# The second layer's early choice in two column groups, ScalarE alone for three accumulator copies, and other widths for two hot experts

## The chip, the cores and the metric

The kernel runs on one core of a Trainium2 chip. A time is the device time of one launch in microseconds (us). The engines of the core work in parallel, each through its own instructions in a fixed order: TensorE (PE; its weight loads are PEld), VectorE (DVE), ScalarE (ACT), GpSimd (POOL) and SyncE (SP, which only issues DMAs here). TensorE accumulates into PSUM; ScalarE and VectorE bring the results into SBUF.

## The reference

Linear attention over 4 x 8 heads of 576 tokens with a head size of 64, then two mixture-of-experts (MoE) layers on the 2304 tokens of 512 values. Each MoE layer chooses one of 8 experts per token, the second with a capacity of 576 tokens per expert:

```python
def _moe_ref(x, w_gate, w1, w2):
    logits = x @ w_gate
    expert_idx = np.argmax(logits, axis=1)
    ...
        xe = x[mask]
        h = np.maximum(xe @ w1[e], 0.0)          # 512 -> 1024
        ye = h @ w2[e]                           # 1024 -> 512
        out[mask] = gate_w[mask, None] * ye

# second layer, the same with
    cap = N // E * 2                             # 576
    for i in range(N):
        e = expert_idx[i]
        if counts[e] < capacity: ...             # later tokens of a full expert give zeros
```

For the inputs that are timed, the first layer's experts have 275, 263, 320, 346, 271, 298, 310 and 221 tokens, the second layer's 477, 159, 320, 248, 144, 524, 259 and 173 (worked out with the reference on its own inputs).

## The kernel before

**Blocks.** All matrix work of a layer is cut into blocks of tokens of one expert, run one after the other by `moe` (L1421). A block of width w has a phase 1 (hidden values, `phase1_prods` L1222, tile `hps`: 8 groups of 12 matmuls, each group called fc 0 to 7) and a phase 2 (`phase2` L1247, accumulators `acc`: again 8 groups of 12). Values are split in a high and a low part and three products are added (`prods`, L1205, lines L1211 to L1213), so 192 matmuls of w columns make a block. In layer one the blocks are 128 (inside the attention stage), 224, 320, 312, 300, 276, 272, 264 and 224 wide, counted 0 to 8. The first layer's rows lie in 23 columns of up to 128 rows: column 0 is block 0, block 5 (276 wide) starts at column 12, block 7 (264) at 18. `LAYOUT2` gives the widths of the second layer in the order of the experts' token counts that are left after an early block of 256 tokens of the "hot" expert, the one with most tokens in the columns that the early choice sees.

**Block forms in layer two.** A block whose width is a multiple of 128 is computed by rows: phase 2 takes the hidden values as the stationary operand and 512 columns of w2 as the moving one (48 matmuls for a width of 256), and its output is scaled by ScalarE and scattered by one DMA per 128 tokens (`still_tile`, L1278). Any other width is "turned": 96 matmuls of w columns, VectorE transposes of the four accumulators, VectorE products with the gate and one scatter on POOL per 32 tokens (`turn_out`, L1374).

**Order of the work around the matmuls.** After each group fc the function `slot` (L1451) issues, in this order: the outputs of the block before (`outs`), a split of one weight tile for what comes next (`feed.pump`: ScalarE makes the high part, L1105, VectorE the low part, L1108), steps of a routing generator, and in phase 2 one step of the next block's input (`xs`). For the last five blocks of layer one a tile of that input is a VectorE transpose (`xw`, L1162), then ScalarE's high part (`xh`, L1195), then VectorE's low part (`xl`, L1199). A generator is run by credit: `run(us)` adds us and steps until the credit is used up; a bare `yield` costs 0.27, `yield PE_WAIT` 1.54.

**The early choice of layer two** (`early(1)`, L861) works on the first 18 columns of the first layer's output in a single group: maximum and one-hot (`chosen`), counts by two matmuls (`prefix`, L615/L616), the hot expert, ranks, one-hot tables (`lo` L929, `high_hot`), a matmul gather of indices (`index`, L666) and the indirect DMAs that fetch the first 256 tokens (L1137). It is stepped in phase 2 of block 7 (0.4 of credit a slot, `THEN0`) and in block 8 (0.7 a slot in phase 1, `THEN1`). The code already has a branch for a second group of columns, which takes the hot expert from the first group and adds ranks by two small matmuls.

**Accumulator copies.** When a block of layer one ends, `evac` (L1314) copies its four accumulators to `yt`: numbers 0 and 2 on ScalarE (L1321), 1 and 3 on VectorE (L1319). Matmuls with an identity and the gate's weights (`yps`, L1341) turn `yt` into rows in the next block's phase 1; ScalarE (`y`, L1345) and VectorE (`l`, L1346) read them, and two PSUM tiles take turns.

Of the kernel before, what the change touches and what calls it, by code (L numbers as in the profile page):

```python
# [27 lines left out]
GROUPS = ((0, 4), (4, 9), (9, 13), (13, 18))  # L28
# [22 lines left out]
TA = 1, WA // 128  # L51


LAYOUT1 = [[224], [320], [312], [300], [276], [272], [264], [224]]
LAYOUT2 = [[256], [256, 268], [320], [260], [176], [160], [144], [256]]
RANKS1 = [0, 1, 2, 3, 4, 5, 6, 7]
RANKS2 = [0, 1, 2, 3, 5, 6, 7, 4]

# [47 lines left out]
def tiles_of(w):  # L106
    return (w + 127) // 128
# [18 lines left out]

L1, L2 = Layout(LAYOUT1, TA[0]), Layout(LAYOUT2, TA[1])
NT = max(L1.nt, L2.nt)
XWMAX = max(w for ws in LAYOUT1 + LAYOUT2 for w in ws)
NCMAX = max(NCOL, L1.cols)  # L130


EARLY = ((GROUPS[1][1],), (TA[0] + L1.base[-2],))
NEARLY = [g[-1] for g in EARLY]


def constants():
# [18 lines left out]
    put("rev", 7 - e)  # L156
    for n in sorted({NCOL, L1.cols, N // 128, *sum(EARLY, ())}):
        put(f"carry{n}", np.tile(np.arange(n) > 0, E))
# [17 lines left out]
class Kernel:  # L176
# [411 lines left out]
    def chosen(self, m, c0, c1, d, oh):  # L588
# [4 lines left out]
        first = self.firsts[m][:, c0:c1]  # L593
        A3 = [128, n, E]
        mx = self.t([128, n], F32, "mx")
        V.tensor_reduce(out=mx, in_=lg, axis=AX.X, op=ALU.max)
        V.tensor_tensor(out=d, in0=lg, in1=bc(mx, 2, A3), op=ALU.subtract)
        yield
        w = self.t(A3, F32, "w")
        V.scalar_tensor_tensor(out=w, in0=d, scalar=0.0, in1=first, op0=ALU.is_equal, op1=ALU.mult)  # L600
        V.tensor_reduce(out=mx, in_=w, axis=AX.X, op=ALU.max)
        yield
        V.tensor_scalar(out=mx, in0=mx, scalar1=0.5, scalar2=None, op0=ALU.max)
        V.tensor_tensor(out=oh, in0=w, in1=bc(mx, 2, A3), op=ALU.is_equal)
        yield PE_WAIT
# [166 lines left out]
    def lead(self):  # L772
# [4 lines left out]
        er = self.er[0] = {}  # L777
        A3, AE = [128, n, E], [128, E, n]
        eq = t(A3, F16, "ohe")
        d = t(A3, F32, "da")  # L780
# [80 lines left out]
    def early(self, m):  # L861


        nc, V, t = self.nc, self.nc.vector, self.t
        groups = EARLY[m]
        ncol = groups[-1]
        er = self.er[m] = {}
        val = (self.tok1, self.slot2)[m][:, 0:ncol]
        oh = t([128, ncol, E], F16, "ohe")
        d = t([128, ncol, E], F32, "da")  # L870
        own = t([128, ncol], F16, "owna")
        sel = t([128, ncol], F32, "sel")
        tl = t([128, ncol], F16, "tla")
        lo = self.xp.tile([128, 128, ncol], F16, tag="lo", name="loa")
        hv = self.rp.tile([128, 2, TA[1], ncol], F16, tag="hva", name="hva")
        hot = t([128, E], F32, "hot0")
        er["sel"], er["d"], er["hot"], er["hot_low"], er["hot_high"] = sel, d, hot, lo, hv
        for c0, c1 in zip((0,) + groups, groups):
            n = c1 - c0
            s = slice(c0, c1)  # L880
            A3 = [128, n, E]
            yield from self.chosen(m, c0, c1, d[:, s], oh[:, s])
            if c0 == 0:
                run, pf = yield from self.prefix(oh[:, s], n)
                key = t([128, E], F32, "key")
                V.scalar_tensor_tensor(
                    out=key, in0=run[:, :, n - 1], scalar=8.0, in1=self.c("rev"), op0=ALU.mult, op1=ALU.add
                )
                top = t([128, 1], F32, "top")
                V.tensor_reduce(out=top, in_=key, axis=AX.X, op=ALU.max)  # L890
                yield
                V.tensor_scalar(out=hot, in0=key, scalar1=top, scalar2=None, op0=ALU.is_equal)
                he = t([128, E], F32, "he")
                V.tensor_tensor(out=he, in0=hot, in1=self.c("e"), op=ALU.mult)
                ordf = t([128, 1], F32, "orda")
                V.tensor_reduce(out=ordf, in_=he, axis=AX.X, op=ALU.add)
                er["ordi"] = t([128, 1], I32, "ordia")
                V.tensor_copy(out=er["ordi"], in_=ordf)
                yield
            w = t(A3, F32, "w")  # L900
            V.tensor_tensor(out=w, in0=oh[:, s], in1=bc(hot, 1, A3), op=ALU.mult)
            with nc.allow_low_precision("zeros and ones"):
                V.tensor_reduce(out=own[:, s], in_=w, axis=AX.X, op=ALU.add)
            yield
            rank = t([128, n], F32, "rank")
            if c0 == 0:
                V.tensor_tensor(out=w, in0=w, in1=pf.rearrange("p e c -> p c e"), op=ALU.mult)
                V.tensor_reduce(out=rank, in_=w, axis=AX.X, op=ALU.add)
            else:
                before = self.psum()[:, 0:c1 + n]  # L910
                nc.tensor.matmul(out=before[:, c1:], lhsT=self.triw, rhs=own[:, s], start=True, stop=True)
                nc.tensor.matmul(out=before[:, 0:c1], lhsT=self.onew, rhs=own[:, 0:c1], start=True, stop=True)
                self.hold = True
                yield
                run = t([128, c1], F32, "runa")
                V.tensor_tensor_scan(
                    out=run, data0=self.c(f"carry{c1}")[:, 0:c1], data1=before[:, 0:c1], initial=0.0,
                    op0=ALU.mult, op1=ALU.add,
                )
                V.tensor_tensor(out=rank, in0=before[:, c1:], in1=run[:, s], op=ALU.add)  # L920
                self.hold = False
            yield
            V.scalar_tensor_tensor(
                out=sel[:, s], in0=rank, scalar=float(WA), in1=own[:, s], op0=ALU.is_lt, op1=ALU.mult
            )
            low, tla = yield from self.low_high(rank, n, "")
            V.tensor_tensor(out=tl[:, s], in0=tla, in1=sel[:, s], op=ALU.mult)
            yield
            V.tensor_tensor(  # L929
                out=lo[:, :, s], in0=self.iotaw[:, :, s], in1=bc(low, 1, [128, 128, n]), op=ALU.is_equal  # L930
            )
            yield 0.1 * n
            self.high_hot(tl[:, s], val[:, s], n, TA[1], hv[:, :, :, s])
            yield PE_WAIT
        yield from self.index(m, er, lo, hv, ncol, TA[1], "a", self.blocks[m][0].gather)
# [375 lines left out]

        return [turn, logits]

    def evac(self, acc, w):  # L1314
        nc = self.nc
        yt = self.yt_tile(w)
        for dc in range(DC):
            if dc % 2:
                nc.vector.tensor_copy(out=yt[:, dc, 0:w], in_=acc[dc][:, 0:w])  # L1319
            else:  # L1320
                nc.scalar.activation(out=yt[:, dc, 0:w], in_=acc[dc][:, 0:w], func=ACTF.Copy)  # L1321
        return yt
# [98 lines left out]
    def moe(self, m, then=None, follow=None, fin=None):  # L1421

        blocks, feed = self.blocks[m], self.feed[m]
# [4 lines left out]
        def run(l, n=99):  # L1428
            for _ in range(n):
                if l:  # L1430
                    l.pop(0)()

        def settle(*gens):
            for g in gens:
                while self.hold:
                    g.step()

        for k, b in enumerate(blocks):
            if m == 0 and k < 1:
                continue  # L1440
            j, w = b.j, b.w
            nb = blocks[k + 1] if k + 1 < len(blocks) else None
            nx = nb or follow
            gen = fin if nb else (then or Steps(iter(())))
            also = then if then and k == len(blocks) - 2 else None
            own, ahead = 8 * j + 8, 8 * j + (12 if nb and nb.j != j else 8)
            if k and nb:
                nb.gather()
# [28 lines left out]
            else:  # L1477
                for fc in range(FC):
# [4 lines left out]
                    elif fc:  # L1483
                        slot(fc % 2 or j == 0 or not nb, own, RATES[m][0] if nb else THEN1)
            run(outs)
            feed.pump(4, own)
            settle(gen)
            self.psum, self.spare = lambda: self.ph.tile([128, 512], F32, tag="h", name="sp"), "h"
# [2 lines left out]
            if rows and not nb and w > 128:  # L1491
                self.nc.gpsimd.drain()
                for t in range(w // 128):
                    acc = self.pa.tile([128, 512], F32, tag="a", name="acc")
# [8 lines left out]
            acc = [self.pa.tile([128, 512], F32, tag="a", name="acc") for _ in range(w // 128 if rows else DC)]  # L1503
# [19 lines left out]
                    xs.extend(nb.x_steps())  # L1523
            if k == 1:
                fin.run()
            settle(gen)
            if also:
                settle(also)
            if rows and m:
                for t in range(w // 128):  # L1530
                    self.still_tile(acc[t], b.rt, b.t0 + t)
            elif rows:
                outs.extend(self.still_rows(acc[0], b.rt, b.t0, b.col))
            elif b.turned:
                outs.extend(self.turn_out(acc, w, b.rt, b.t0))
            else:
                yt = self.evac(acc, w)
                for t in range(tiles_of(w)):
                    outs.extend(self.out_tile(m, yt, w, b.rt, b.t0, t, b.col))
            run(xs)  # L1540
# [167 lines left out]
    def run(self):  # L1708
        nc, tc, ctx = self.nc, self.tc, self.ctx
        self.pools()  # L1710
        self.hold = False
        self.tags, self.lp = {"hv", "pv"}, None
        self.view, self.turning = 0, 1
        self.er, self.rt = [{}, {}], [{}, {}]
# [222 lines left out]
```

## Time and profile before

| what | value |
|---|---|
| median of 3 runs | 582.75 us (581.17 to 585.8) |
| profiled execution, its own time | 584.3 us |
| its span, first to last instruction | 582.5 us |
| TensorE busy | 552.8 us, 95% of the span |
| VectorE / ScalarE / GpSimd busy | 57% / 42% / 31% |
| mean granted TensorE clock | 0.986 of full |

The busy time of TensorE counts pipelined matmuls as one stretch, so short waits between two matmuls hide in it. In the timeline a number in brackets with an arrow is the idle time of the engine before the instruction, and what ended it. In the table of stretches (block 5's phase 2 is 233.8 to 245.8, block 8's two phases 300.5 to 319.3 and 319.3 to 336.5) PEclk is the granted clock of TensorE, as a share of full.

### The profile page before, as it was taken

To read this page: it belongs to the slowest core of one execution; us is meant where nothing else is said; L and a number is where in the kernel's file an instruction comes from. 1 tells how busy PE (TensorE), PEld (TensorE's weight loads), DVE (VectorE), ACT (ScalarE), POOL (GpSimd) and SP (SyncE) were. 2 spreads that over 40 slices of the span, in tenths; PEclk is the share of its full clock that TensorE was granted. 3 is DMA by queue.
4 is the path that set the end of the run, shared out by engine and by line. 5 is a ranking of instruction groups with operands and counts; after the bars stand their busy time and mean duration, and the time that the engine had idled before them with its cause. 6 is when DMAs were issued, how large, how long until landed. Compare 5 with 4: busy or idle time off the path is not lost.

```text
span 582.5 us, 10758 instructions
## 1 busy us (share of the span) xinstructions
PE 552.8 (95%) x4130; PEld 525.1 (90%) x4130; DVE 330.2 (57%) x741; ACT 243.8 (42%) x421; POOL 182.4 (31%) x187
## 2 busy tenths in 40 slices
PE   8898898999999999999998999999999999999995
PEld 6887776998999999999987998989899999989994
DVE  0466983467867576767688586275147662211370
ACT  0456622436455555564645342244243532111440
POOL 1032225066625243433000101203322726543341
PEclk8999899999999999999999898999999999999998
DMA  9996746055556465656555434236234655768631
GB/s 305 399 381 217 264 144 193 3 178 168 179 172 205 157 203 172 213 176 200 175 181 166 134 111 167 72 93 234 88 101 153 202 188 177 257 238 265 242 127 39
DMA packets 34231, 106.89 MB, mean 184 GB/s; under 512 B 6665, under 2 KB 6795, under 8 KB 34172
## 3 DMA queue, kind: packets, MB, share of 16 engines
q1 hardware_dynamic: 24432, 81.90, 41.8%
q0 software_dynamic: 7072, 19.48, 10.7%
q10 hardware_dynamic: 2667, 4.75, 2.4%
q8 instruction: 34, 0.56, 0.4%
q14 instruction: 26, 0.20, 0.1%
HBM read 91.77 MB, written 14.60 MB: 183 GB/s over the span
## 4 chain that ended last, share of the span: by engine, by line
PE 69%; DVE 15%; issue 6%; ACT 5%; DMA 2%; POOL 1%; POOLq 0%; SPq 0%; ACTq 0%; DVEq 0%; another core or an unknown queue 0%
PE hps L1211 8%; PE hps L1212 8%; PE hps L1213 8%; PE acc L1211 7%; PE acc L1212 7%; PE acc L1213 7%; PE acc L1209 5%; PE hps L1209 4%; PE yps L1341 3%; DVE w1l L1108 3%; DVE w2l L1108 2%; PE xps L1187 2%; PE kv L368 2%; PE o L400 2%; PE sp L666 1%
## 5 line engine op out<-in xcount | busy, mean ns | idle before, releaser
L1211 PE MATMUL hps<-xh,w1h 128*128 128x256 f32 (+9 forms) x480 | 141.5, 295 | 1.0 <-ACT xh L1195 0.6
L1212 PE MATMUL hps<-xl,w1h 128*128 128x256 f32 (+9 forms) x480 | 139.0, 290 | 0.6 <-DVE xl L1199 0.5
L1213 PE MATMUL hps<-xh,w1l 128*128 128x256 f32 (+9 forms) x480 | 138.6, 289 | 0.0
L1232 ACT ACTIVATE hh<-hps 128x256 fp32r<-128x256 f32 (+12 forms) x144 | 54.4, 380 | 150.1 <-PE hps L1213 97.6
L1211 PE MATMUL acc<-hh,w2h 128*128 128x224 f32 (+8 forms) x352 | 104.6, 297 | 0.1
L1212 PE MATMUL acc<-hl,w2h 128*128 128x224 f32 (+8 forms) x352 | 103.0, 293 | 0.8 <-issue 0.8
L1213 PE MATMUL acc<-hh,w2l 128*128 128x224 f32 (+8 forms) x352 | 103.1, 293 | 0.0
L1211 PEld LDWEIGHTS hps<-xh,w1h 128*128 128x128 f32 x480 | 91.0, 190 | 3.0 <-issue 1.5
L1212 PEld LDWEIGHTS hps<-xl,w1h 128*128 128x128 f32 x480 | 91.1, 190 | 1.7 <-DVE xl L1199 1.3
L1213 PEld LDWEIGHTS hps<-xh,w1l 128*128 128x128 f32 x480 | 91.1, 190 | 0.0
L1234 DVE SCALAR_TENSOR_TENSOR hl<-hps,hh 128x256 fp32r<-128x256 f32 (+9 forms) x120 | 51.7, 436 | 63.7 <-ACT hh L1232 54.7
L1148 POOL DMA_INDIRECT xg<-x1d,gi x54 | 54.9, 1016 | 77.5 <-DVE xw L1162 63.5
L1108 DVE TENSOR_TENSOR w2l<-raw,w2h 128x1024 fp32r<-128x1024 f32 x52 | 66.2, 1276 | 19.2 <-ACT w2h L1105 18.1
L1396 POOL DMA_INDIRECT out_dram<-y,gi x44 | 50.5, 1149 | 70.9 <-DVE y L1392 56.8
L1108 DVE TENSOR_TENSOR w1l<-raw,w1h 128x1024 fp32r<-128x1024 f32 x52 | 64.0, 1248 | 13.6 <-ACT hh L1232 7.8
L1213 PEld LDWEIGHTS acc<-hh,w2l 128*128 128x128 f32 x352 | 67.2, 191 | 0.9 <-issue 0.9
L1211 PEld LDWEIGHTS acc<-hh,w2h 128*128 128x128 f32 x352 | 67.3, 191 | 0.3
L1212 PEld LDWEIGHTS acc<-hl,w2h 128*128 128x128 f32 x352 | 67.3, 191 | 0.2 <-issue 0.2
L1105 ACT ACTIVATE w2h<-raw 128x1024 fp32r<-128x1024 f32 x52 | 54.6, 1053 | 5.6 <-ACT y L1345 4.8
L1105 ACT ACTIVATE w1h<-raw 128x1024 fp32r<-128x1024 f32 x52 | 53.4, 1049 | 0.6 <-DMA raw<-in_moe_w_dram 0.5
L1137 POOL DMA_INDIRECT xg<-x2d,gi x21 | 20.0, 952 | 48.3 <-DVE gi L677 33.9
L1195 ACT ACTIVATE xh<-xps 128x512 fp32r<-128x512 f32 (+7 forms) x23 | 11.7, 512 | 45.3 <-PE xps L1187 31.2
(315 smaller groups left out, 818.9 us busy)
## 6 DMA issues: line engine op xcount, KB each, us to landing
raw<-in_moe_w_dram SPq DMA_DIRECT2D x104, 512.0 KB
w<-in_moe_w_dram SPq DMA_DIRECT2D x24, 512.0 KB
x1d<-xs POOLq DMA_DIRECT2D x4, 1056.0 KB
qkv<-in_k_dram SPq DMA_DIRECT2D x8, 512.0 KB
qkv<-in_v_dram SPq DMA_DIRECT2D x8, 512.0 KB
qkv<-in_q_dram SPq DMA_DIRECT2D x8, 512.0 KB
x2d<-y ACTq DMA_DIRECT2D x15, 256.0 KB
xg<-x1d,gi POOLq DMA_INDIRECT x59
```

What stands on the lines that cost most here:

```text
L1105: self.nc.scalar.activation(out=h, in_=t, func=ACTF.Copy)
L1108: self.nc.vector.tensor_tensor(out=l, in0=t, in1=h, op=ALU.subtract)
L1137: self.nc.gpsimd.indirect_dma_start(out=xg[:n], out_offset=None, in_=(self.X1, self.X2)[m][0:rows], in_offset=bass.IndirectOffsetOnAxis(ap ...
L1148: self.nc.gpsimd.indirect_dma_start(out=xg[:, g], out_offset=None, in_=(self.X1, self.X2)[m].rearrange("n (q x) -> (n q) x", q=4), in_offs ...
L1209: nc.tensor.matmul(out=out, lhsT=a[0], rhs=b[0], start=start, stop=stop)
L1211: nc.tensor.matmul(out=out, lhsT=a[0], rhs=b[0], start=start, stop=False)
L1212: nc.tensor.matmul(out=out, lhsT=a[0], rhs=b[1], start=False, stop=False)
L1213: nc.tensor.matmul(out=out, lhsT=a[1], rhs=b[0], start=False, stop=stop)
L1232: nc.scalar.activation(out=hh[:, fc, :], in_=ps, func=ACTF.Relu)
L1234: nc.vector.scalar_tensor_tensor(out=hl[:, fc, :], in0=ps, scalar=0.0, in1=hh[:, fc, :], op0=ALU.max, op1=ALU.subtract)
L1341: nc.tensor.matmul(out=ps[:n, j, :], lhsT=yt[:, dc, 128 * t:128 * t + n], rhs=self.iwg[:, dc, :], start=True, stop=True)
L1396: self.nc.gpsimd.indirect_dma_start(out=out, out_offset=bass.IndirectOffsetOnAxis(ap=rt["si4"][:, g - g0, t0 + t:t0 + t + 1].bitcast(U32), ...
```

## The change

The early choice of layer two takes its 18 columns in two groups, 12 and then 6. It is stepped in phase 2 of blocks 5, 6 and 7 instead of 7 alone, and a group begins only when the outputs of its columns have been issued (`self.done`). The hot expert is now the one that leads in the first 12 columns. `settle` steps the generators in turn until none holds a matmul result. ScalarE alone copies the accumulators of blocks 6, 7 and 8. Layer two's hot expert gets a rest of 268 (was 256) and the next expert 256 and 224 (was 256 and 268). The constant table gains the row of 96 values that a scan over 12 columns needs.

```diff
-LAYOUT2 = [[256], [256, 268], [320], [260], [176], [160], [144], [256]]
+LAYOUT2 = [[268], [256, 224], [320], [260], [176], [160], [144], [256]]
...
-EARLY = ((GROUPS[1][1],), (TA[0] + L1.base[-2],))
+EARLY = ((GROUPS[1][1],), (TA[0] + L1.base[-4], TA[0] + L1.base[-2]))
...
@@ early
             A3 = [128, n, E]
+            while self.done < c1:
+                yield
             yield from self.chosen(m, c0, c1, d[:, s], oh[:, s])
...
-    def evac(self, acc, w):
+    def evac(self, acc, w, alone=False):
...
-            if dc % 2:
+            if dc % 2 and not alone:
                 nc.vector.tensor_copy(out=yt[:, dc, 0:w], in_=acc[dc][:, 0:w])
...
@@ moe
         def settle(*gens):
-            for g in gens:
-                while self.hold:
-                    g.step()
+            while self.hold:
+                for g in gens:
+                    if g and self.hold:
+                        g.step()
...
-            also = then if then and k == len(blocks) - 2 else None
+            also = then if then and len(blocks) - 5 < k < len(blocks) - 1 else None
...
             run(outs)
+            if m == 0:
+                self.done = b.col
             feed.pump(4, own)
...
-            settle(gen)
-            if also:
-                settle(also)
+            settle(gen, also)
...
-                yt = self.evac(acc, w)
+                yt = self.evac(acc, w, k > len(blocks) - 4)
...
-        self.hold = False
+        self.hold, self.done = False, 0
```

## Rows read from the trace of the kernel before

**Rows 1.** The page, busy time of each engine, share of the span and instructions.
```profile
PE 552.8 (95%) x4130; PEld 525.1 (90%) x4130; DVE 330.2 (57%) x741; ACT 243.8 (42%) x421; POOL 182.4 (31%) x187
```

**Rows 2.** Stretches: us, busy us (instructions) of PE, PEld, DVE, ACT, POOL; PEclk, DMA, GB/s.
```profile
233.80:245.80 12.00, 12.00 (x98) 12.00 (x97) 8.59 (x12) 6.26 (x9) 5.97 (x6) 1.00 0.65 204
...
300.50:319.30 18.80, 15.31 (x140) 14.49 (x139) 16.38 (x50) 9.78 (x21) 0.00 (x0) 1.00 0.53 173
319.30:336.50 17.20, 16.81 (x142) 16.38 (x141) 9.67 (x27) 7.08 (x13) 1.93 (x2) 0.90 0.49 157
```

**Rows 3.** Timeline of DVE in block 5's phase 2: start, us, instruction, [idle before].
```profile
236.49 1.22 DVE L1108 TENSOR_TENSOR w1l<-raw,w1h 128x1024 fp32r<-128x1024 f32 x1
237.63 0.70 DVE L1162 STREAM_TRANSPOSE xw<-xg 128x512 f32<-128x512 f32 x1
239.13 0.75 DVE L1199 SCALAR_TENSOR_TENSOR xl<-xw,g,xh 128x512 fp32r<-128x512 f32 x1 [0.79 <-ACT xh L1195]
240.08 1.23 DVE L1108 TENSOR_TENSOR w1l<-raw,w1h 128x1024 fp32r<-128x1024 f32 x1 [0.20 <-ACT w1h L1105]
...
245.57 0.36 DVE L1199 SCALAR_TENSOR_TENSOR xl<-xw,g,xh 128x64 fp32r<-128x64 f32 x1 [0.42 <-issue]
...
247.66 0.79 DVE L1319 COPY yt<-acc 128x276 f32<-128x276 f32 x2
```

**Rows 4.** Timeline of PE: the second matmul of blocks 6 and 7.
```profile
245.98 0.39 PE L1212 MATMUL hps<-xl,w1h 128*128 128x272 f32 x1
...
273.73 0.39 PE L1212 MATMUL hps<-xl,w1h 128*128 128x264 f32 x1 [0.35 <-DVE xl L1199]
```

**Rows 5.** Groups of DVE instructions, 291 to 320 us: busy us, mean ns.
```profile
L929 DVE TENSOR_TENSOR loa<-iotaw,low 128x2304 f16<-128x2304 f16 x1 | 1.4, 1420 | 0.0
...
L597 DVE TENSOR_TENSOR da<-aux,mx 128x144 f32<-128x144 f32 x1 | 0.3, 308 | 0.0
...
L886 DVE SCALAR_TENSOR_TENSOR key<-run,ct 128x8 f32<-128x8 f32 x1 | 0.2, 157 | 0.0
```

**Rows 6.** Waits of PE, 240 to 336.5 us: us in total, times, longest.
```profile
PE yps L1341 <- DVE l L1346: 1.8, 2, 1.4
PE yps L1341 <- DVE yt L1319: 1.1, 1, 1.1
PE sp L666 <- DVE hva L659: 0.9, 1, 0.9
```

**Rows 7.** Timelines of ACT and DVE: accumulator copies of block 7.
```profile
300.49 0.65 ACT L1321 ACTIVATE yt<-acc 128x264 f32<-128x264 f32 x2
...
304.21 0.76 DVE L1319 COPY yt<-acc 128x264 f32<-128x264 f32 x2
```

**Rows 8.** Busy time by stretch: 3.3 us early in block 8's phase 2.
```profile
320.10:323.40 3.30, 3.30 (x18) 3.30 (x17) 1.81 (x9) 0.01 (x1) 1.93 (x2) 0.50 0.57 186
```

**Rows 9.** Timelines of POOL and PE: gathers, and what reads them.
```profile
98.15 0.95 POOL L1137 DMA_INDIRECT xg<-x1d,gi  x1 [0.30 <-issue]
...
101.92 1.05 POOL L1179 TENSOR_TENSOR xr<-xg 128x512 f32<-128x512 f32 x1 [0.42 <-DMA xg<-x1d,gi]
...
320.44 0.98 POOL L1137 DMA_INDIRECT xg<-x2d,gia  x1 [46.80 <-DMA raw<-in_moe_w_dram]
...
326.23 0.63 PE L1187 MATMUL xps<-ct,xg 128*128 128x128 f32 x4
```

**Rows 10.** Busy time by stretch: 224 columns; layer two's 256, 256, 268 (two phases).
```profile
329.80:333.80 4.00, 4.00 (x38) 4.00 (x37) 4.00 (x5) 2.44 (x5) 0.00 (x0) 1.00 0.64 207
368.90:392.20 23.30, 23.30 (x153) 21.30 (x152) 13.46 (x39) 9.40 (x17) 3.99 (x4) 1.00 0.30 95
392.20:416.20 24.00, 24.00 (x158) 21.55 (x157) 9.36 (x15) 9.37 (x18) 4.89 (x5) 1.00 0.50 170
416.20:428.10 11.90, 11.90 (x97) 11.90 (x96) 2.97 (x7) 3.54 (x9) 5.90 (x6) 1.00 0.40 123
428.10:441.50 13.40, 13.40 (x110) 13.19 (x109) 7.73 (x12) 5.77 (x8) 1.84 (x2) 1.00 0.45 138
```

## Prediction

> **What bounds the kernel now.** First the busy table: TensorE is busy 95% of the span, VectorE 57% [rows 1]. So only two kinds of edit can pay: less matmul work, or an end to stretches in which TensorE waits. The table of stretches shows where these are. Phase 2 of block 5 is full: 12.00 of 12.00 us [rows 2]. In phase 1 of block 8 TensorE is busy 15.31 of 18.80 us and VectorE 16.38: there VectorE is the bound [rows 2]. The list of waits puts names to it: 1.1 us until VectorE copies an accumulator, 1.4 us (and twice a little) until VectorE's gate sums free a PSUM tile, 0.9 us until the one-hot table of the early choice is there [rows 6]. And behind that last wait 3.3 us of phase 2 ran at a granted clock of 0.50, that is at 1.2 GHz of 2.4 [rows 8].
>
> The second thing to see is how close VectorE is to being the bound in the earlier blocks, though it is busy only 8.59 of 12.00 us there [rows 2]. The timeline of block 5's phase 2 shows a chain: weight split 236.49, transpose 237.63, then VectorE stands 0.79 us until ScalarE has made the high part, low part 239.13, next weight split 240.08 [rows 3]. One input tile takes 3.6 us (240.08 - 236.49), three tiles and their weights nearly the whole phase. The last low part begins at 245.57 and takes 0.36, so it ends at 245.93; the matmul that reads it starts at 245.98 [rows 3, 4]. One block later that matmul already waits, 0.35 us [rows 4]. So what is put into VectorE's queue in phase 2 of blocks 5 and 6 ahead of these parts comes out as a wait of TensorE, except what fits into the 0.8 us holes.
>
> **The change part by part.** I add up differences against the profiled execution (584.3 us, span 582.5; 1.55 above the median of 582.75) and apply them to the median.
>
> *Early choice, first group.* Credit of 0.4 a slot fixes what is issued where. In block 5: fc 0 two steps (four operations on 12 x 8 = 96 values), fc 1 one step, fc 5 the two matmuls, the scan and an add, fc 6 two tiny ones, fc 7 six. Durations: 144 values take 0.308 us, 8 values 0.157 [rows 5], so 96 values about 0.26 (estimate, on that line). Ahead of the last low part and not in a hole: 4 x 0.26 + (0.16 + 0.26) + 0.6 (scan and add) = 2.1 us. The matmul had no slack, so block 6 starts its second matmul 2.1 us late. Behind it, fc 7's operations (1.2 us) and the weight split precede block 5's accumulator copies on VectorE, which are still shared there: 247.66 [rows 3] becomes some 251.2, the first copy is done at 251.6, and `yps` wants it after two groups of 1.5 us behind 248.0, at 251.1: 0.45 us more. In block 6: fc 0 two operations (0.55), fc 1 seven small ones (7 x 0.16 = 1.1), fc 2 the one-hot table, 1.42 x 12/18 = 0.95 us [rows 5], of which 0.8 fits the hole, fc 5 two (0.3): 0.55 + 1.1 + 0.15 + 0.3 = 2.1 us, all of it on top of the 0.35. Sum for the first group: **+4.65 us**. Bounds: 0, if the chain has slack that I don't see, and 6.
>
> *Second group.* Six columns, in block 7's phase 2, whose next block has two input tiles and no wait at its start: nothing. What is left of it (ranks, tables, 1.75 us of VectorE with a table of 0.5) runs in block 8's fc 1 and fc 2. Two more pairs of small matmuls and one pair fewer: **+0.3 us** of TensorE (the pair of before and one `x18` gather stay).
>
> *Copies by ScalarE alone.* Two copies take 0.65 us on ScalarE, 0.76 on VectorE [rows 7]; VectorE began its own only at 304.21, 3.7 us after ScalarE's 300.49 [rows 7], because early steps stood before them. Four in a row on ScalarE end some 1.3 us after the block's end, and `yps` comes after two groups of 1.3 us: the wait of 1.1 us goes, **-1.1**. ScalarE has nothing else due until the first `hh`. At block 8's own end the same takes some **-0.4** of the small waits.
>
> *Block 8's other waits.* The gate sums of the second output tile stand in VectorE's queue behind the first w2 split and the steps of fc 1. These steps are 1.75 us now against 1.4 before, while TensorE comes 1.1 us earlier: by my walk through the two queues the sums are done at about 309.9 and TensorE wants the tile at 307.95, a wait of 2.0 in place of 1.4: **+0.6**. The index matmuls move from fc 7 to fc 4 and find their table: **-0.9**. With no wait in front of phase 2 the clock should stay: 3.3 us at half rate lose half, **-1.6**.
>
> *What is late next.* The input steps of layer two follow four slots after the gather is issued. The gather moves forward, but its index is read on VectorE behind the queue, at about 316.4; POOL takes it at some 317.2 (0.8 allowed). How long it takes to land is not shown directly: a product that waited for a gather issued at 98.15 began at 101.92, 3.8 us [rows 9], and the one issued at 320.44 was read at 326.23 without a wait, so at most 5.8 [rows 9]. TensorE comes to these transposes at about 320.3, the rows at 321.0 to 323.0: a wait of 0.7 to 2.7, I take **+1.5**, nearer to the gather that is seen waited for.
>
> *Widths.* The hot expert of the first 12 columns is the one with 524 tokens (299 there against 260 of the one with 477; over 18 columns it was 436 against 446), so 268 and 480 fit exactly and no extra round runs. 224 columns run 36 matmuls in 4.0 us, 0.111 each [rows 10] (38 touch the stretch); 268 run 96 in 11.9, 0.124. The hot rest was 23.3 us and becomes 2 x 11.9 + 0.9 (next block's input) = 24.7: +1.4. The second block was 11.9 + 13.4 = 25.3 and becomes 2 x 10.7 + 1.5 = 22.9: -2.4. A third input tile of 12 tokens moves from the second 256-block to the early block, +0.4 - 0.6. Sum **-1.2**; bounds -2 and 0. The hot rest is turned now: four transposes on VectorE and nine scatters on POOL for two, and two fewer at the next. VectorE is busy 9.36 of 24.0 us there and POOL 4.89 [rows 10], and the turned 268-block of before hands over without a wait: nothing, and 2 us at most if that cover were gone. The longer constant table is 49 KB more in the attention stage: nothing to 0.3.
>
> Sum: 4.65 + 0.3 - 1.1 - 0.4 + 0.6 - 0.9 - 1.6 + 1.5 - 1.2 = +1.85, so about **584.5 us**.
>
> **A rule beside the clock.** The row shows the clock at 0.50 behind a wait of 0.9 us and a run of very short matmuls [rows 6, 8], while waits of 1.1 and 1.4 us earlier in the block left it at 1.00 [rows 2, 6]. The Trainium skill, "TensorE: Matmul & The Clock Gate", section "HAM oscillation — how this bites in real kernels", ties a fall of the clock to long idle gaps of TensorE; by that rule the new waits of 2 us could not lower the clock, and the sum would stay as it is. The trace disagrees in its one case, so I price a fall at 1.6 us for each new wait in the rivals.
>
> **The rivals.**
> *Faster: VectorE has room after all (chance 0.2).* If the first group's steps in blocks 5 and 6 fit between the chain's parts and the gather lands in time, only gains are left: -1.1 - 0.4 - 0.9 - 1.6 - 1.2 + 0.3 = -4.9, and -6.3 if the wait for the gate sums goes too: 576.4 to 577.9. For it: VectorE is idle 3.4 us of block 5's phase 2 [rows 2]. Against: most of that idle time lies where the queue's order can't use it [rows 3].
> *Slower by over 1%: the new waits pull the clock down (0.1).* Waits of over 2 us at 246, 273 and 320 us, each followed by a stretch at half clock: 3 x 1.6 on top of 1.85, with the gather at its later bound (+1.2): +7.9, 590.6. It decides as soon as a wait at a block's start is as costly as the 0.9 us one. For it: that one [rows 6, 8]; against: the waits of 1.1 and 1.4.
> *The early choice does not get shorter (0.1).* If block 8 stays bound by VectorE, with the gate sums waiting 3 us and the clock falling as before, -0.9 - 1.6 are lost: +4.4, 587.1.
> The forecast has 0.6, with a range of its own from 581 to 588.
>
> **How the numbers follow.** 1% is 5.8 us, about what a measurement of this kernel tells from no change: under 576.9 or over 588.6. Faster takes about a third of the first rival and hardly anything else: 0.09. Slower takes the second rival and some of the forecast's upper end: 0.11. Same: 0.80. The range leaves out the far ends of both: 578 to 590.
>
> **What would show it.** In the profile after: a wait of some 2 us of `hps` L1212 on VectorE's `xl` at the start of blocks 6 and 7; no wait of `yps` on `yt`; the wait of L666 on `hva` gone; granted clock 1.00 through block 8; a wait for the gather at the first transposes of layer two; layer two's hot rest some 24.7 us long. Wrong it would be if blocks 6 and 7 start without a wait, or if the second layer's blocks differ by more than 2 us in sum.

## The result, and the profile after

The changed kernel took 590.44 us (median of 4 runs, 587.53 to 592.6) against 582.26 us (median of 4): a ratio on record of **1.011**, interval 1.0065 to 1.0155, where the two medians alone would give 1.014. A second measurement gave 1.0069 (1.0031 to 1.0107). So by the two ratios it is 4 to 6 us slower, by these medians 8; the forecast was 1.85 us slower, no change within 1%. The profiled execution of after took 587.53 us (span 585.5), the fastest of its four. An execution more than 1.5% above the fastest of its kernel counts as slow: the ratios leave such runs out, and the profiles of `e1_copies`, `e4_after`, `e7_xg6` and `e8_late` are of slow ones, so what is read from them below is single stages, with their clock. Lines of the changed kernel's code stand two further down: 1197 to 1201 are the input parts, 1213 to 1215 the matmuls, 1343 `yps`, 1348 `l`.

The page, busy time of each engine (compare [rows 1]):

```profile
PE 549.7 (94%) x4180; PEld 523.8 (89%) x4180; DVE 334.0 (57%) x761; ACT 244.0 (42%) x425; POOL 190.1 (32%) x192
```

TensorE has 50 matmuls more, yet 3.1 us less busy time; what is lost is in its waits. The list of waits of PE from 240 us, the middle of block 5's phase 2, through block 8, against [rows 6]:

```profile
PE hps L1213 <- ACT xh L1197: 4.8, 2, 3.6
PE yps L1343 <- DVE l L1348: 2.4, 3, 1.8
PE yps L1343 <- DVE yt L1321: 0.8, 1, 0.8
PE xps L1189 <- DMA xg<-x2d,gia: 0.7, 1, 0.7
```

The wait for the index table (`hva`) is gone, the one on `yt` is now another (block 5's copies, in block 6's phase 1; block 7's make none wait), `l` grew a little. New and largest are the waits of the first matmuls of blocks 6 and 7 on the input's high part, 4.8 us together. The stretches (us; busy of PE, PEld, DVE, ACT, POOL; PEclk; DMA; GB/s), in order block 5 phase 2, block 6 phase 2, block 8 phases 1 and 2, against [rows 2]:

```profile
233.10:246.90 13.80, 12.56 (x101) 12.24 (x99) 10.57 (x22) 6.05 (x9) 5.99 (x6) 1.00 0.56 180
...
263.80:279.50 15.70, 12.16 (x98) 11.94 (x96) 13.10 (x23) 5.98 (x9) 6.72 (x5) 0.99 0.48 157
...
307.50:324.50 17.00, 15.23 (x141) 14.63 (x141) 12.75 (x41) 9.60 (x21) 0.90 (x1) 1.00 0.59 196
324.50:340.50 16.00, 14.96 (x141) 14.58 (x139) 8.27 (x22) 7.74 (x14) 1.03 (x2) 1.00 0.54 180
```

Block 5's phase 2 went from 12.0 to 13.8 us and block 6's to 15.7, while block 8 lost 3.0 us over its two phases (18.86 + 17.15 to 16.99 + 16.02). The two delayed starts in the timeline of PE, against [rows 4]:

```profile
246.89 0.39 PE L1213 MATMUL hps<-xh,w1h 128*128 128x272 f32 x1 [1.24 <-ACT xh L1197]
...
279.53 0.59 PE L1213 MATMUL hps<-xh,w1h 128*128 128x264 f32 x1 [3.57 <-ACT xh L1197]
```

The second is a microsecond more than the 2.1 us of steps and the old wait of 0.35 would make. The timeline of DVE in front of it, to be read against [rows 3], shows both causes:

```profile
268.85 0.17 DVE L639 TENSOR_TENSOR high<-rank,low 128x12 f32<-128x12 f32 x1
269.05 0.17 DVE L641 TENSOR_SCALAR tl<-high 128x12 f16<-128x12 f32 x1
269.26 0.17 DVE L929 TENSOR_TENSOR tla<-tl,sel 128x12 f16<-128x12 f16 x1
269.47 0.71 DVE L1164 STREAM_TRANSPOSE xw<-xg 128x512 f32<-128x512 f32 x1
270.10 0.98 DVE L931 TENSOR_TENSOR loa<-iotaw,low 128x1536 f16<-128x1536 f16 x1
...
273.06 0.70 DVE L1164 STREAM_TRANSPOSE xw<-xg 128x512 f32<-128x512 f32 x1
274.56 2.29 DVE L1201 SCALAR_TENSOR_TENSOR xl<-xw,g,xh 128x512 fp32r<-128x512 f32 x1 [0.79 <-ACT xh L1197]
276.77 1.21 DVE L1110 TENSOR_TENSOR w1l<-raw,w1h 128x1024 fp32r<-128x1024 f32 x1
277.91 0.79 DVE L658 TENSOR_TENSOR hva<-iotaw,tla 128x24 f16<-128x24 f16 x1
```

And the timeline of POOL in the same stretch:

```profile
270.45 1.44 POOL L1150 DMA_INDIRECT xg<-x1d,gi  x1 [15.64 <-DVE xw L1164]
...
275.23 1.06 POOL L1181 TENSOR_TENSOR xg<-xg 128x512 f32<-128x512 f32 x1
277.17 1.50 POOL L1181 TENSOR_TENSOR xg<-xg 128x384 f32<-128x384 f32 x1 [0.88 <-DMA xg<-x1d,gi]
```

The last three of seven small steps and the one-hot table stand ahead of the parts, as predicted. But a full `xl`, 0.75 us elsewhere, took 2.29, and `hva`, 0.16 elsewhere, took 0.79, just while GpSimd multiplied gathered rows. GpSimd got there by the same delay: its gather waited for a buffer until VectorE's transpose at 269.47 had read it.

Behind the wait of 3.57 us the clock fell, and it stayed at full rate behind those of 1.24 and 1.77 (the latter on `l`, in block 8). The first row below is that stretch; the other three are layer two's hot rest and the second expert's blocks of 256 and 224, against [rows 10]; [rows 8] has no counterpart in this profile:

```profile
280.00:283.40 3.40, 3.40 (x20) 3.40 (x20) 1.50 (x2) 1.97 (x6) 0.00 (x0) 0.62 0.28 111
...
372.10:396.30 24.20, 24.20 (x201) 24.20 (x200) 14.22 (x43) 8.91 (x16) 5.89 (x6) 1.00 0.39 121
396.30:419.60 23.30, 23.30 (x154) 21.26 (x153) 12.02 (x22) 8.44 (x15) 10.20 (x9) 1.00 0.43 145
419.60:442.50 22.90, 22.90 (x206) 22.72 (x205) 10.25 (x18) 8.91 (x17) 7.62 (x8) 1.00 0.43 138
```

Between the two profiles (3.0 us of span) the stages differ by: start of block 1 -0.7 us, blocks 1 to 4 +0.3, blocks 5 to 8 **+4.4**, layer two to the end of the 320-block **-3.0**, its last five blocks +2.1. The last lies in blocks that the change leaves as they were: phase 2 of the 260-, 176- and 160-blocks, here for after and then for experiment `e11` below, which has the same blocks there:

```profile
483.40:497.70 14.30, 13.09 (x106) 12.52 (x105) 2.54 (x6) 2.27 (x4) 7.93 (x8) 1.00 0.52 177
507.20:520.60 13.40, 11.79 (x75) 10.49 (x74) 0.40 (x2) 1.08 (x3) 5.77 (x6) 1.00 0.55 192
529.30:540.10 10.80, 9.98 (x74) 9.57 (x74) 0.63 (x3) 1.32 (x4) 2.98 (x4) 1.00 0.73 240
```

```profile
474.90:487.40 12.50, 12.50 (x107) 12.31 (x106) 2.59 (x6) 2.27 (x4) 7.91 (x8) 1.00 0.73 230
496.90:507.40 10.50, 10.50 (x74) 10.25 (x73) 0.32 (x2) 1.19 (x3) 5.75 (x6) 1.00 0.80 257
516.10:525.80 9.70, 9.70 (x74) 9.50 (x73) 0.60 (x3) 1.13 (x3) 3.08 (x4) 1.00 0.92 322
```

38.5 us against 32.7 for the same work. Of the difference, 3.6 us are gaps of TensorE that the trace puts down to nothing ("issue"); the rest lies in stretches that count as busy. Such gaps were in every trace of the first two studies (35.5 us and more; before: 36.5) and in none of the last, on another chip.

### The profile page after: what moved, and what is told of

The parts are those of the page before. It is cut to its first block, busy times and chain, and to the rows that moved or that the text cites. A ratio compares the mean times of both kernels' runs of the same rounds, so it can differ in the third digit from the quotient of the medians.

```text
span 585.5 us, 10894 instructions
## 1 busy us (share of the span) xinstructions
PE 549.7 (94%) x4180; PEld 523.8 (89%) x4180; DVE 334.0 (57%) x761; ACT 244.0 (42%) x425; POOL 190.1 (32%) x192
## 4 chain that ended last, share of the span: by engine, by line
PE 65%; DVE 13%; issue 6%; DMA 6%; ACT 6%; POOL 1%; SPq 1%; POOLq 0%; ACTq 0%; DVEq 0%; another core or an unknown queue 0%
PE hps L1213 9%; PE hps L1214 8%; PE hps L1215 8%; PE acc L1213 7%; PE acc L1214 7%; PE acc L1215 7%; PE acc L1211 5%; PE hps L1211 4%; PE yps L1343 4%; DVE w2l L1110 2%; DVE w1l L1110 2%; PE xps L1189 2%; DMA qkv<-in_q_dram 2%; DMA qkv<-in_v_dram 2%; ACT w2h L1107 1%
## 5 line engine op out<-in xcount | busy, mean ns | idle before, releaser
L1213 PE MATMUL hps<-xh,w1h 128*128 128x224 f32 (+9 forms) x480 | 142.1, 296 | 5.6 <-ACT xh L1197 5.4
L1214 PE MATMUL hps<-xl,w1h 128*128 128x224 f32 (+9 forms) x480 | 139.2, 290 | 0.2
L1215 PE MATMUL hps<-xh,w1l 128*128 128x224 f32 (+9 forms) x480 | 138.8, 289 | 0.0
L1234 ACT ACTIVATE hh<-hps 128x224 fp32r<-128x224 f32 (+12 forms) x144 | 54.1, 379 | 154.4 <-PE hps L1215 104.6
L1213 PE MATMUL acc<-hh,w2h 128*128 128x224 f32 (+8 forms) x384 | 112.6, 293 | 0.1
L1215 PE MATMUL acc<-hh,w2l 128*128 128x224 f32 (+8 forms) x384 | 111.2, 290 | 0.7 <-issue 0.7
L1214 PE MATMUL acc<-hl,w2h 128*128 128x224 f32 (+8 forms) x384 | 111.2, 290 | 0.4 <-issue 0.4
L1398 POOL DMA_INDIRECT out_dram<-y,gi x51 | 58.4, 1145 | 97.8 <-DVE y L1394 83.1
L1236 DVE SCALAR_TENSOR_TENSOR hl<-hps,hh 128x224 fp32r<-128x224 f32 (+9 forms) x120 | 51.6, 434 | 61.3 <-ACT hh L1234 50.6
L1110 DVE TENSOR_TENSOR w2l<-raw,w2h 128x1024 fp32r<-128x1024 f32 x52 | 66.2, 1275 | 20.0 <-ACT w2h L1107 18.6
L1213 PEld LDWEIGHTS acc<-hh,w2h 128*128 128x128 f32 x384 | 72.6, 189 | 1.0 <-issue 0.8
L1215 PEld LDWEIGHTS acc<-hh,w2l 128*128 128x128 f32 x384 | 72.6, 189 | 0.5 <-issue 0.5
L1214 PEld LDWEIGHTS acc<-hl,w2h 128*128 128x128 f32 x384 | 72.6, 189 | 0.3 <-issue 0.2
L1110 DVE TENSOR_TENSOR w1l<-raw,w1h 128x1024 fp32r<-128x1024 f32 x52 | 64.5, 1259 | 14.2 <-ACT w1h L1107 13.6
L1139 POOL DMA_INDIRECT xg<-x2d,gi x21 | 19.8, 944 | 47.6 <-DVE gi L677 34.8
L1211 PE MATMUL acc<-hh,w 128*128 128x176 f32 (+2 forms) x192 | 29.1, 301 | 2.4 <-issue 2.3
```

The lines of the kernel that those rows point to most:

```text
L1110: self.nc.vector.tensor_tensor(out=l, in0=t, in1=h, op=ALU.subtract)
L1139: self.nc.gpsimd.indirect_dma_start(out=xg[:n], out_offset=None, in_=(self.X1, self.X2)[m][0:rows], in_offset=bass.IndirectOffsetOnAxis(ap ...
L1211: nc.tensor.matmul(out=out, lhsT=a[0], rhs=b[0], start=start, stop=stop)
L1213: nc.tensor.matmul(out=out, lhsT=a[0], rhs=b[0], start=start, stop=False)
L1214: nc.tensor.matmul(out=out, lhsT=a[0], rhs=b[1], start=False, stop=False)
L1215: nc.tensor.matmul(out=out, lhsT=a[1], rhs=b[0], start=False, stop=stop)
```

## The experiments

They ran in three studies, each on a chip of its own with the kernel before beside it (584.4, 585.0 and 579.4 us); only ratios and stages are compared across them. The expectations count the phases of blocks 1 to 8 from 0: 8 and 9 are block 5's, 10 and 11 block 6's, 12 is block 7's phase 1, 14 and 15 are block 8's; 27 is the 260-block's phase 2. A table of stages stands at the end of this section.

**Copies alone, `e1_copies`** (the kernel before with this):

```diff
-                yt = self.evac(acc, w)
+                yt = self.evac(acc, w, k > len(blocks) - 4)
```

> Before plus one part alone: ScalarE copies all four accumulators of blocks 6 to 8. Theory 'chain' (the slowdown sits in VectorE steps of the first group of the early choice, issued ahead of the low parts of the next block's input): this part is innocent, block 8's wait for yt (1.1 us before) goes and the time falls by 0.5 to 1.5 us, 581 to 582 where before has 582.3. Rival 'ScalarE late' (four copies in a row hold up the hidden values of the next block): slower by 1 to 3 us, with waits of TensorE on hh or acc behind block ends.

Ratio 0.9966 (0.9935 to 0.9998): 2.0 us gained (0.1 to 3.8 by the interval), where 1.5 was predicted. The wait on `yt` in block 8 is gone. The wait on the index table is still there, 0.93 us, yet the clock behind it stayed at 1.00 and block 8's phase 2 took 15.2 us in place of 17.15.

**Widths alone, `e2_widths`** (the kernel before; one group, but the hot expert is read from its first 12 columns, so that the widths fit):

```diff
-LAYOUT2 = [[256], [256, 268], ...
+LAYOUT2 = [[268], [256, 224], ...
...
-                    out=key, in0=run[:, :, n - 1], ...
+                    out=key, in0=run[:, :, TA[0] + L1.base[-4] - 1], ...
```

> Before plus one part alone: the widths 268 and 256, 224, with the early choice in one group of 18 columns; so that the widths fit, the hot expert is taken from the counts over the first 12 columns inside that single group. Theory 'chain': the widths give 1 to 1.5 us, so 581. Rival 'second layer' (the turned hot rest costs more in the blocks behind it): slower by 1 to 4 us, to be seen in the blocks after the hot rest.

Ratio 1.0025 (0.9988 to 1.0063): no gain. The blocks themselves are shorter as predicted (hot rest to second expert 70.9 us against 72.6), but the trace lost more than that again among the narrow blocks: 19.1 us in place of 13.6 in phase 27, with the clock down for 6.8 of them.

**One group, `e5_one_group`** (the changed kernel without the two groups; copies and widths stay, the hot expert is read as in `e2_widths`), and **`e4_after`**, the changed kernel itself on that chip:

```diff
-EARLY = ((GROUPS[1][1],), (TA[0] + L1.base[-4], TA[0] + L1.base[-2]))
+EARLY = ((GROUPS[1][1],), (TA[0] + L1.base[-2],))
...
-            also = then if then and len(blocks) - 5 < k < len(blocks) - 1 else None
+            also = then if then and k == len(blocks) - 2 else None
```

> The changed kernel without its two groups: copies by ScalarE alone and the new widths, the early choice in one group as before (hot expert by the first 12 columns). Theory 'chain': all of the slowdown is in the two groups, so this is faster than before by 1.5 to 3 us (579 to 581), and blocks 6 and 7 start with waits of 0 and 0.35 us. Rivals 'ScalarE late' and 'second layer': 584 or more.

> The changed kernel again, on the chip of the other three. Theory 'chain': 587 to 592, waits of TensorE at the start of blocks 6 and 7 of 1.2 and 2.5 to 3.6 us again. Theory 'clock' (the executions of the changed kernel spread from 587 to 593 because its waits let the granted clock fall in some of them): in this profile another number of 3.4 us stretches at half clock than the one at 280 us, and a time that goes with it by about 1.6 us each.

Ratios 1.0002 (0.9967 to 1.0036) and 1.0069 (1.0031 to 1.0107). The two groups cost 0.67%, 3.9 us; blocks 5 to 8 are 6.3 us shorter without them (116.3 against 122.6). The gain of 1.5 to 3 us over the kernel before that was expected of `e5_one_group` did not come: its blocks 5 to 8 are 2 us shorter than before, but the copies and the widths together don't show in its time.

The two profiles of the changed kernel differ by 7.6 us of span: 3.5 lie ahead of block 1, 2.3 in the narrow blocks and 1.5 in blocks 5 to 8, where the second one has a fall of the clock in block 8's phase 1 (0.91 over 18.6 us) beside the one in block 7 (0.90 in both). So in these two the clock makes the smaller part of the spread.

**Steps in the holes, `e6_holes`** (the changed kernel):

```diff
-                if also:
-                    also.run(THEN0)
                 if fc:
                     run(xs, 1)
+                if also:
+                    also.run(THEN0)
```

> The changed kernel with the early choice's steps issued behind the step of the next block's input instead of ahead of it, so that on VectorE they follow the transpose and fall into its wait for ScalarE's high part. If VectorE's chain of input parts sets the starts of blocks 6 and 7 (my theory), each of the three holes of 0.8 us in a phase 2 takes steps for nothing: the waits of 1.24 and 3.57 us shrink to some 0.3 and 1 to 2, phases 9 to 12 lose 2 to 4 us together, the time is some 0.5% under the changed kernel. If the delay came from GpSimd's products alone, the waits change by the shift of these products only, under 1 us. If the run is set by the clock, the time follows the number of stretches at half clock and not the waits.

Ratio 0.9991 (0.9955 to 1.0026), some 1% under the changed kernel's two ratios. Its timeline of DVE shows how:

```profile
269.11 0.70 DVE L1164 STREAM_TRANSPOSE xw<-xg 128x512 f32<-128x512 f32 x1
269.74 0.13 DVE L925 SCALAR_TENSOR_TENSOR sel<-rank,owna 128x12 f32<-128x12 f32 x1
...
271.06 0.17 DVE L929 TENSOR_TENSOR tla<-tl,sel 128x12 f16<-128x12 f16 x1
271.15 0.75 DVE L1201 SCALAR_TENSOR_TENSOR xl<-xw,g,xh 128x512 fp32r<-128x512 f32 x1
...
275.37 1.05 DVE L1201 SCALAR_TENSOR_TENSOR xl<-xw,g,xh 128x512 fp32r<-128x512 f32 x1 [0.79 <-ACT xh L1197]
```

The steps now lie between transpose and `xl`, where VectorE stood for 0.79 us. Phases 2 of blocks 5 and 6 are 1.0 and 2.3 us shorter, and the second `xl` takes 1.05 in place of 2.29, because the transpose, and with it GpSimd's gather, comes earlier. The start of block 7 still waits 1.3 us. In this trace a fall of the clock hit block 8's phase 1 (0.83 over 19.8 us), so the kernel's profile shows less of the gain than its runs.

**Gathers earlier, `e7_xg6`** (the changed kernel; the tag `xg` with six buffers):

```diff
-... tag="xg", name="xg", bufs=4) ...
+... tag="xg", name="xg", bufs=6) ...
```

> The changed kernel with six gather buffers in place of four, so that GpSimd's gathers and products come earlier. If the extra 1.1 us at block 7's start is VectorE stretched by GpSimd's product (xl 2.29 us in place of 0.75, hva 0.79 in place of 0.16), these durations return to normal there when the product lies elsewhere, the wait of 3.57 us falls to some 2.0 to 2.5, without a fall of the clock behind it: about 2 us under the changed kernel. The rest (the steps' own time in VectorE's queue, 2.1 us a block) stays. If the stretch is not the products' doing, xl stays at 2.3 us where the product has gone.

Ratio 1.0272 (1.0216 to 1.0327), 1.6 to 2.0% over the changed kernel's two where a gain of 2 us was expected. But it shows what the stretched instructions do when GpSimd is elsewhere. GpSimd had nothing to do any more in block 6's phase 2, and the same stretch of DVE reads:

```profile
289.20 0.71 DVE L1164 STREAM_TRANSPOSE xw<-xg 128x512 f32<-128x512 f32 x1
290.70 0.75 DVE L1201 SCALAR_TENSOR_TENSOR xl<-xw,g,xh 128x512 fp32r<-128x512 f32 x1 [0.79 <-ACT xh L1197]
...
292.80 0.16 DVE L658 TENSOR_TENSOR hva<-iotaw,tla 128x24 f16<-128x24 f16 x1
```

`xl` is back at 0.75 and `hva` at 0.16; that phase took 13.90 us at full clock in place of 15.77. So of the 3.73 us by which it had grown over 12.04, **1.87 are GpSimd's doing and 1.86 the steps' own**. The loss is elsewhere: phases 1 of blocks 3, 4 and 5 grew by 3.6, 3.9 and 4.7 us, in block 3 with a wait of `yps` on `l` of 3.2, in 4 and 5 with the clock down (0.92 and 0.91); layer two to its 320-block grew by 5.6. Why there stays open.

**From block 7 on, `e8_late`** (the changed kernel):

```diff
-            also = then if then and len(blocks) - 5 < k < len(blocks) - 1 else None
+            also = then if then and k == len(blocks) - 2 else None
```

> The changed kernel with the early choice stepped from block 7's phase 2 on, as before the change; the two groups stay. If the steps in blocks 5 and 6 cost the time, phases 9 to 12 return to the lengths without groups (12.05, 15.25, 12.04, 15.1 to 15.3: 8 us less than in the changed kernel); phase 2 of block 7 and block 8 then hold both groups and may take 2 to 5 us more. Sum: 3 to 6 us under the changed kernel, 583 to 586. If instead two groups cost by their number of operations wherever they stand, block 8 gets longer by as much as blocks 6 and 7 get shorter, and the time stays near 589.

Ratio 0.9976 (0.9943 to 1.001). Phases 9 to 12 (block 5's phase 2 to block 7's phase 1) took 12.05, 15.23, 12.04 and 14.65 us: all of the loss is gone from there. Block 8's phase 2 pays, 21.18 us (clock 0.97). The waits of PE from block 5's phase 2 to the start of layer two, all but one of 1.3 us on `l` in that phase:

```profile
PE yps L1343 <- DVE l L1348: 2.6, 3, 1.3
PE sp L913 <- DVE owna L905: 1.4, 1, 1.4
PE yps L1343 <- ACT yt L1323: 1.2, 1, 1.2
```

**Groups without the copies, `e3_groups`** (the changed kernel with `evac(acc, w)` as before, so that VectorE copies its half again).

> The changed kernel with the accumulator copies shared between ScalarE and VectorE again. If the copies are worth their predicted 1.5 us apart from the groups, block 8's phase 1 has a wait on yt again and the time is 590 to 591, some 1.5 us over the changed kernel. If VectorE's queue ahead of the copies is longer now (steps at the end of blocks 6 and 7), the copies by ScalarE are worth more, 2 to 4 us. If they matter only where no groups are, no difference.

Ratio 1.0111 (1.007 to 1.0151). Block 7's phase 1 is 1.1 us and block 8's 2.7 us longer than in the changed kernel's trace, but there the clock fell further (0.84 and 0.83, against 0.90 and 1.00). Against the changed kernel's 1.0069 the times differ by some 2.5 us, inside both intervals, and against its 1.011 not at all. The wait on `yt` that was expected to come back in block 8 did not: VectorE starts its copies 1.2 us into that phase (312.77, the phase from 311.52), where in the kernel before it was 3.7 us, because two early steps stand between in place of ten. So with two groups the removal of that wait needs no copies by ScalarE, and what they are worth beside the groups is not shown.

**The last three**, with the way out that the earlier ones point to. `e9_from6` is `e6_holes` with

```diff
-            also = then if then and len(blocks) - 5 < k < len(blocks) - 1 else None
+            also = then if then and len(blocks) - 4 < k < len(blocks) - 1 else None
```

`e10_one_holes` is `e1_copies` with the edit of `e6_holes`, and `e11_one_holes_w` is `e10_one_holes` with the two edits of `e2_widths`.

> The changed kernel with two edits: the early choice stepped from block 6 on (not from block 5), and its steps behind the step of the next block's input. If the chain of input parts with its holes of 0.8 us sets the starts, phase 9 returns to 12.05, phase 11 is some 12.9 in place of 15.77, the starts of blocks 6 and 7 wait 0 and under 1 us, and no fall of the clock follows: phases 8 to 15 some 115 to 117 us in place of 122.6, the time 581 to 584, 1% under the changed kernel and no worse than the kernel before. If two groups cost by their work wherever it stands, block 8 takes it back: 586 to 589.

> The kernel before with ScalarE alone copying for three blocks and the steps behind the input's step; one group, old widths. In block 7's phase 2, the only one with steps here, the next block has two input tiles and no wait at its start, so by the chain theory the place of the steps is worth nothing: as the copies alone, 0.3% under the kernel before, 581 to 583. If VectorE's queue as a whole is what counts, 1 to 2 us less.

> The same with the new widths of layer two (the hot expert by the counts of the first 12 columns, in the single group). If the widths are worth their 1.2 to 2 us in the end, 579.5 to 582, under the kernel with old widths. If the gain is given back in the later, narrow blocks (the 260-block's second phase took 14.2 to 14.3 us with the new widths in five traces of seven and more in two, 12.7 and 13.6 with the old), there is no difference or a loss of up to 2 us.

Ratios 0.9971 (0.994 to 1.0003), 0.9964 (0.9927 to 1.0002) and 0.9956 (0.9923 to 0.999), in this order. `e9_from6` keeps both groups and all other parts of the change, and the loss is gone; its phase 11 took 12.79 us where 12.9 was expected. Its waits of PE from block 5's phase 2 to 340 us, 6 us into layer two, where the one on `oh` lies, as in the kernel before:

```profile
PE sp L913 <- DVE owna L905: 2.3, 1, 2.3
PE yps L1343 <- DVE l L1348: 1.7, 3, 1.0
PE sp L615 <- DVE oh L604: 0.5, 1, 0.5
PE hps L1213 <- ACT xh L1197: 0.2, 1, 0.2
```

The starts wait 0.2 us, and a new wait of 2.3 at the second group's small matmul has come into block 8's phase 1. `e11_one_holes_w`, one group, beats the kernel before by 2.5 us (0.6 to 4.5). The three can't be told apart, so two groups in this order are shown neither to cost nor to gain. Old and new widths (`e10`, `e11`) can't be told apart there either.

Lengths of stages in us, from the first matmul of one to that of the next (P1, P2: phases; "to 320": layer two from its early block through the 320-block; "narrow": the five blocks behind it):

| kernel | 5 P2 | 6 P1 | 6 P2 | 7 P1 | 8 P1 | 8 P2 | blocks 5-8 | to 320 | narrow |
|---|---|---|---|---|---|---|---|---|---|
| before | 12.05 | 15.24 | 12.04 | 15.26 | 18.86 | 17.15 | 118.3 | 134.6 | 111.4 |
| after | 13.81 | 16.88 | 15.77 | 16.17 | 16.99 | 16.02 | 122.6 | 131.6 | 113.4 |
| e5_one_group | 12.05 | 15.25 | 12.04 | 15.04 | 17.46 | 16.80 | 116.3 | 133.3 | 112.7 |
| e6_holes | 12.85 | 16.79 | 13.45 | 15.42 | 19.70 | 15.11 | 120.4 | 131.6 | 112.1 |
| e3_groups | 13.81 | 17.21 | 15.78 | 17.25 | 19.71 | 15.15 | 125.9 | 131.5 | 112.8 |
| e9_from6 | 12.05 | 15.24 | 12.79 | 15.00 | 16.90 | 17.53 | 116.3 | 133.8 | 107.7 |
| e10_one_holes | 12.06 | 15.23 | 12.04 | 14.65 | 17.45 | 16.80 | 115.6 | 134.6 | 107.4 |
| e11_one_holes_w | 12.06 | 15.25 | 12.02 | 14.95 | 17.46 | 15.18 | 114.2 | 133.4 | 107.7 |

## Why the prediction held, and where it was off

**By the time** it was close: 590.44 us lies just above the 590 at which the stated range ends and above the 588.6 from which it would call the change slower; the ratio 1.011 on the 582.75 of the prediction gives 589.2, and the second measurement, 1.0069, gives 586.8.

**Direction and mechanism** were right: the early choice's first group, put ahead of the input's parts in VectorE's queue, delays the starts of blocks 6 and 7. What was predicted as their sign is there, on `xh` in place of `xl`: the high part is the first thing that the delayed transpose holds up.

**The term of the first group was mis-sized**, 4.65 us. Its pieces: block 6's start 2.1, measured 1.76 (13.81 - 12.05); the wait on `yt` 0.45, measured 0.81, in block 6's phase 1 altogether +1.64; block 7's start 2.1 on top of the 0.35, measured 3.73. With the clock's fall behind it (block 7's phase 1, +0.9) and 0.3 less in block 5's phase 1 the stretch lost 7.7 us. The steps' own 1.86 us in block 6 had been costed at 2.1: that arithmetic was good. What it left out is that VectorE's own instructions get longer when its queue moves against GpSimd's. Block 6's phase 1 has it too: ahead of the copies that `yps` waits for, a weight split at 247.81 took 1.85 us in place of 1.22, beside two products of GpSimd (247.53, 2.39 together). The trace of before shows this at the very matmul from which the 0.35 was read. Its last low part (timeline of DVE):

```profile
272.11 0.30 DVE L1162 STREAM_TRANSPOSE xw<-xg 128x128 f32<-128x128 f32 x1
272.80 0.88 DVE L1199 SCALAR_TENSOR_TENSOR xl<-xw,g,xh 128x32 fp32r<-128x32 f32 x1 [0.39 <-ACT xh L1195]
```

and the timeline of POOL beside it:

```profile
272.80 0.83 POOL L1179 TENSOR_TENSOR xg<-xg 128x384 f32<-128x384 f32 x1 [2.30 <-DMA xg<-x1d,gi]
```

32 columns in 0.88 us, while in the changed kernel, where GpSimd was done, they took 0.25. A duration that is several times that of its like was the row to stop at.

**The wider pattern.** In the trace of after, 92 weight splits that overlap no product of GpSimd take at most 1.27 us; of the 12 that overlap one, five take 1.40 to 3.98 and seven no more than the others. So an overlap can stretch them and need not; what decides it is not shown. Transposes of 256 and 128 columns took the same with and without a product beside them (0.43, 0.30), and so did `hl`, which reads one operand from PSUM (0.39). The Trainium skill, "SBUF — State Buffer", section "Who interferes with whom", says that a VectorE instruction with two SBUF inputs contends with a GpSimd instruction that reads SBUF, and that one with at most one SBUF input does not, outside the two-port performance modes. The trace agrees as to which ones are stretched: `xl`, the splits and `hva` read two tiles in SBUF, the transposes one.

**The terms of block 8** came out in this profile as walked through: the wait on `yt` is gone (predicted -1.1; `e3` shows that the groups alone would have removed it), `l` 1.77 us where 2.0 was predicted, the index table's wait gone, the fall of the clock gone, the wait for the gather 0.74 where 1.5 was taken from 0.7 to 2.7. Their sum with the copies was predicted at -1.9, measured -3.0 over both phases. The term of the clock, -1.6, is luck in part: with the same wait of 0.93 us on the index table the clock fell in the phase behind it in `e5` and `e10` (0.90, 16.8 us) and stayed at 1.00 in `e1` and `e11` (15.2 us), and the changed kernel itself had a fall in block 8's phase 1 in its second profile (0.91), behind the 1.77 us on `l`.

**Copies** -1.5, measured -2.0. **Widths** -1.2: the hot rest and the second expert gained 2.2 us in the profile (72.6 to 70.4), a microsecond more than predicted, but no timed pair shows it: +0.25% alone, +0.36% between `e1` and `e5`, -0.08% between `e10` and `e11`, each within its interval. Gaps in the narrow blocks, which differ by several us between executions, cover it. Whether the widths bring these gaps on is not settled; on the chip without gaps both widths had narrow blocks of 107.4 to 107.7 us.

**By timed runs** of one study the parts are +3.9 (groups), -2.0 (copies) and +2.1 (widths, from `e1` to `e5`), which add up, as they must, to the measured +4.0, each with an uncertainty of 2 to 3 us; the forecast had +4.55 for the groups (4.65 + 0.3 + 0.6 - 0.9 - 1.6 + 1.5), -1.5 and -1.2. The groups' net is near because two errors in it cancel: from `e5` to after the stages up to block 7 grew by 7.6 us, 3 more than costed, while block 8 and layer two to its 320-block gave 3.0 back where 0.1 was reckoned.

**The rivals.** VectorE has no room in the queue's order as written, but nearly enough in another: `e6` and `e9` show that the holes which [rows 3] has take the steps. The rival of three new falls of the clock came true once, at the longest wait (3.57 us, and 3.58 in `e3` and `e4`, with 0.84 and 0.90 behind it), and not at the others; a median near its 590.6 was reached by another way. Block 8 did get shorter.

## What to carry to other kernels

When steps are put into an engine's queue, price the chain that stands behind them, and place them in that chain's own holes: here the same steps behind the transpose in place of ahead of it are worth some 1% of the kernel. Then ask which other engine moves along with the delayed chain, and what it will lie beside: look in the trace for instructions of one form that are far longer than their like, and see what ran beside them. A gain of 2 us in the middle needs more than a few runs where later stages differ by that much from one execution to the next.

## What the runs showed of the hardware

VectorE's instructions with two inputs in SBUF took up to 3.98 us in place of 1.22, and 2.29 in place of 0.75, beside a GpSimd product, though seven of 12 splits beside one kept their time; transposes, with one input, kept theirs (0.43, 0.30). On the chip of the last study TensorE had no gaps in the narrow blocks (32.7 us for three phases), elsewhere 35.5 us and more for the same instructions, with nothing named that they waited for; the cause is not known. Two more gather buffers, which let GpSimd run ahead, cost the changed kernel 1.6 to 2.0%. Behind one and the same wait of 0.93 us the clock of TensorE fell to its lower level in some executions (`e5`, `e10`) and not in others (`e1`, `e11`).
